# A 32-head attention block gated by a Mish MLP on one NeuronCore: four more places for the last W2 pieces, three first W1 pieces, and a reordered tail

## The chip, the core and the metric

The kernel runs on one core of a Trainium2 chip. The metric is the device time of one execution, in microseconds (us). A core has a TensorE (PE in the profile, with its weight loads as PEld), a VectorE (DVE), a ScalarE (ACT), a GpSimd (POOL) and a SyncE (SP), each with its own instruction queue that runs in order. SP issues nearly all DMAs here, so an SP instruction that waits holds back every DMA behind it. TensorE writes to PSUM, eight banks of 128 x 512 f32; everything else lies in SBUF tiles whose places are reused.

## The reference

```python
def _A_ref(x, wqkv, wo):                      # attention, 32 heads of 32
    q, k, v = ...                             # (x @ wqkv), split and transposed
    p = _softmax(jnp.einsum("bhqd,bhkd->bhqk", q, k) * (Dh ** -0.5))
    o = jnp.einsum("bhqk,bhkd->bhqd", p, v)
    return o.transpose(0, 2, 1, 3).reshape(B, S, D) @ wo

def _B_ref(x, w1, b1, w2):                    # dense, Mish, dense
    h = x @ w1 + b1
    return (h * jnp.tanh(softplus(h))) @ w2

x = A_x                                       # 1 x 2048 x 1024, f32
xn = _layernorm(x)
return x + _A_ref(xn, wqkv, wo) * silu(_B_ref(xn, w1, b1, w2))   # F = 3584
```

## The kernel before

The work is f32 throughout, and a product of two f32 matrices is made of three matmuls of rounded parts (high x high, high x low, low x high, the table `THREE`), so every operand is split first: ScalarE copies the high part, and VectorE or GpSimd subtracts it to leave the low part (`copy` L282, `low` L290). A matmul that needs the low part of its left operand comes third of its three.

The kernel has three phases. First come layernorm, the projections to Q, K and V, and the presplit W1 and W2, written to DRAM (lines up to 782; the scores of head 0 start there too). Then attention and MLP run together, L785 to L1426: five streams yield matmuls (scores for the row maxima `s`, scores for the exponentials `t`, first MLP layer `h` L1076, second MLP layer `y` L1217, and `p_stream`, the output projection `op` L1357), and the class `Plan`, a list scheduler with costs written by hand, decides at build time in which order each engine's instructions stand. Last comes a tail written by hand, L1429 to L1522.

Places are rings in the plan. `p` has 6 tiles of 128 x 2048 for exponentials (`PS`); an exponential's tile is given back when both its sum (POOL, L939) and its product with V (`pv`, L958; for the last two tiles the sum is a matmul, `zp`, L996) have used it. `w2` has 3 places for pieces of W2 (`W2S`), `w1` has 3 for pieces of W1. The MLP is made in units `U` and row chunks of 512; the second layer uses a Strassen-like scheme with 7 blocks `j` for a pair of units, two half-tiles `s` each, summed by VectorE into `yacc` (L1243). Two pieces of W2 serve a block, so the last pair of units uses pieces 378 to 391, blocks y_0 to y_6.

`p_stream` begins the projection inside the plan: it loads `wo` raw (`wr0` to `wr3`), splits it, loads the first row chunk's attention output (`or0`, `or1`, into `p` tiles, split into `xo`), and yields the eight output tiles of chunk 0 in two halves of the contraction, k = 0 to 3 and then k = 4 to 7. The head outputs go to DRAM in `ot` (L1018), the MLP outputs of each chunk in `ys` (L1284); the last chunk's `ys` store waits for the last `ot` store.

The tail works through chunks c = 0 to 3 of four row tiles t. Chunk 0's matmuls are in the plan already; for c = 1 to 3 each row tile takes two groups (dh = 0, 1) of 24 matmuls (`p_mm`). For them the attention output of the chunk is loaded (`new_o`, `oraw`) and split (`split_o`, `ohl` for odd chunks, `xo` for even ones). The MLP output is loaded (`y_load`, `yp`), its seven blocks are combined by seven POOL additions (`y_total`, L1465; done earlier for chunk 0), `silu` runs on ScalarE, and `end` multiplies the PSUM result by the gate (L1477), adds x (L1478) and stores it (L1482). The bank of a group is reused by the group one chunk later, once `end` has read it. ScalarE and VectorE run these in program order: a `silu` that waits for `y_total` holds back the copies behind it.

```python
    op_ = pool(ph, "op", 8)                   # L1430, over mlp and yacc
    yp = pool(ph, "yp", 2, side="right")      # L1433
    ...
    silu(0)                                   # L1492
    for k in range(4):
        split_o(1, k)                         # the other four are interleaved with end(t, dh), t < 4
```

Of the kernel before, what the change touches and what calls it, by code (L numbers as in the profile page):

```python
# [9 lines left out]
F32 = mybir.dt.float32  # L10
# [8 lines left out]
P = 128  # L19
KT = D // P  # L20
# [11 lines left out]

MM, PV = 0.22667, 0.8587

GROUPS, ZP = (4, 4, 4, 4), 2

LEAD, LATE = 8, 4.0

# [191 lines left out]
def body(ctx: ExitStack, tc: tile.TileContext, x, wqk, wv, wo, w1, b1, w2, out):  # L230
# [7 lines left out]
    def pool(stack, name, bufs, side="left", **kw):  # L238
        return stack.enter_context(tc.tile_pool(name=name, bufs=bufs, side=side, reuse_waits="tile", **kw))
# [363 lines left out]
    def load_head(h, parts=range(3)):  # L603
        r = slice(h % 4 * DH, h % 4 * DH + DH)
        q, k = qst[h % 3], kst[h % 3]
        if h > 2:
            move(q[96:98, :], zeros[0:2, :])
        elif h:
# [150 lines left out]
    for f in range(2 * KT):  # L759
        for c in range(NC):  # L760
            qk_group(f, c if f < 2 * KT - 1 else (c + 1) % NC)
            while todo and todo[0][0] <= f * NC + c:
                todo.pop(0)[1]()
            if c == 0 and f + 1 < 2 * KT:
                qk_split(f + 1)
                if f + 2 < 2 * KT:
                    later.at(1, lambda f=f + 2: qk_load(f))
            if f == 8 and c == 0:
                load_head(0)
            if f == 15 and c == 0:  # L770
# [14 lines left out]
    stk = pool(att0, "stk", 1, side="right")  # L785
    ps_a = psum(att0, "ps_a", 1)
    ph = ExitStack()
    mlp = pool(ph, "mlp", 1)
# [12 lines left out]
    def op(*args, **kw):  # L801
        return plan.add(Op(*args, **kw))
# [238 lines left out]
    def w1_op(n):  # L1041
        def emit(at):
            load_w1(n)
        w1_ops[n] = op("SP", 0.1, emit=emit, take=["w1"], bytes_=P * KT * P * 4)

    def w2_op(m, need=()):
        def emit(at):
            w2t[m] = mlp.tile([P, 2, 512], F32R, tag=f"w2{at['w2']}", name=f"w2_{m}")
# [12 lines left out]
    def h_stream():  # L1061
        for n in range(NC * FT):
            c, f = divmod(n, FT)
            if f == 0 and c + 1 < NC:
                xc_op(c + 1)
            t = {}
            i = 0
            for k in range(KT):
                m_ = 2 * n + k // 4
                if k % 4 == 0 and m_ + 2 < 2 * NC * FT:  # L1070
                    w1_op(m_ + 2)
                for a, b in THREE:
                    def mm(at, n=n, c=c, k=k, a=a, b=b, i=i, t=t, m_=m_):
                        if i == 0:
                            t["h"] = bank(at, f"h{n}")
                        nc.tensor.matmul(t["h"], w1t[m_][:, a, k % 4], xts_[c][:, b, k], start=i == 0, stop=i == 3 * KT - 1)  # L1076
                    last = i == 3 * KT - 1
                    due = n + (i + 1) / 24 - (AHEAD if n >= NC * FT - 2 else 0)
                    m = Op("PE", MM, key=tile_time * due, emit=mm,
                           need=([w1_ops[m_]] if n else []) + ([xc_ops[c, k // 2 * 2]] if c else []),  # L1080
                           take=["d", "b", "h"] if i == 0 else [],
                           give=(["w1"] if i % 12 == 11 else []) + (["xc"] if last and f == FT - 1 else []))
# [112 lines left out]
            act_ops[u, "z", 0].need.append(act_ops[u, "z", 1])  # L1195

    made_by, gs = {}, {}
    yacc = mlp.tile([P, 7, 2, 512], F32, name="yacc")

    def y_stream():  # L1200
        for m in range(W2S):
            w2_op(m, [m_there[0, 3]])
        free, freed = {}, [0]
        for B in range(0, NC * U, 2):
            c, b = divmod(B, U)
            done = {}
            for j, (kind, half) in enumerate(YSEQ):
                t = {}
                for n, (v, s) in enumerate(ORDER):
                    m_ = 7 * B + 2 * j + v  # L1210
                    for i, (p, q) in enumerate(THREE):
# [20 lines left out]
                        if "w2" in give and W2S + (at_ := freed[0]) < NC * U * 7:  # L1232
                            w2_op(W2S + at_)
                        freed[0] += "w2" in give
                        if not last:
                            continue

                        def y_add(at, j=j, s=s, b=b, t=t):
# [3 lines left out]
                            else:  # L1242
# [37 lines left out]

    def y_store(c, done):
        def store(j):
            return op("SP", 0.1, need=[done[j, i] for i in range(2)] + ([stored[H - 1]] if c == NC - 1 else []),
                      bytes_=P * 1024 * 4, emit=lambda at: nc.sync.dma_start(ys[c][:, j], yacc[:, j]))  # L1284

        return {j: store(j) for j in range(7)}

# [72 lines left out]
    def p_stream():  # L1360
# [57 lines left out]

    plan.take_now("w1")
    plan.take_now("w1", 1)  # L1420
    plan.take_now("xc")
    plan.take_now("mx", 1)
    loaded[1] = None
# [9 lines left out]
    yp = pool(ph, "yp", 2, side="right")  # L1433
    oraw = {}

    def new_o(c, k):
# [20 lines left out]

    def y_load(c, js):
        for j in js:
            yt[c, j] = yp.tile([P, 2, 512], F32, tag=f"y{j}", name=f"yp{c}_{j}", bufs=2 if j in BLOCK.values() else 1)  # L1460
            nc.sync.dma_start(yt[c, j], ys[c][:, j])

    def y_total(c):
# [9 lines left out]
    def end(t, dh):  # L1473
        c, s = divmod(t, 4)
        y = yt[c, BLOCK[s // 2, dh]][:, s % 2]
        r = slice(dh * 512, dh * 512 + 512)
        nc.vector.tensor_tensor(y, ps[t, dh], y, ALU.mult)  # L1477
        nc.vector.tensor_tensor(xt[t][:, r], xt[t][:, r], y, ALU.add)  # L1478
# [86 lines left out]
```

## Time and profile before

| | before |
|---|---|
| runs, us | 3377.39, 3377.81, 3380.06; median 3377.81 |
| profiled execution, us | 3378.12 |
| its span, us | 3376.3 (1.8 us of the execution lie around it) |
| DVE, ACT, POOL busy, us | 2505.0, 2059.6, 2741.2 |
| mean granted TensorE clock | 0.996 |

The span runs from the first to the last instruction. PE's time and its waits stand in the prediction's quotes. The granted clock is the share of full speed that TensorE was given; in a stretch of length L with mean clock c, (1 - c) x L is about what the lower clock cost.

### The profile page before, as it was taken

Reading aid. Unit: us, or ns where it says so; the run is one execution under the profiler, and the core shown is the slowest. Engines: PE = TensorE matmul, PEld = TensorE weight load, DVE = VectorE, ACT = ScalarE, POOL = GpSimd, SP = SyncE. Lnnn points to the kernel's source line nnn. Section 1 sums busy time; section 2 is a strip of 40 time slices with the busy share of each in tenths; the row PEclk is TensorE's granted clock in tenths of the full one; section 3 lists DMA queues with packets and bytes.
Section 4 is the critical chain, followed back from the end, with each engine's and each line's share of the span. In section 5 each row is a group of like instructions: output and inputs, shape, how many; then the busy total and the mean of one; then the engine's idle time right before and its main releaser. Section 6 shows DMA issues by size and latency. Waiting matters only on the chain. (4 is left out here: it accounts for less than half of the span.)

```text
span 3376.3 us, 47946 instructions
## 1 busy us (share of the span) xinstructions
PE 3334.9 (99%) x17123; PEld 2454.0 (73%) x17123; DVE 2505.0 (74%) x4126; ACT 2059.6 (61%) x3523; POOL 2741.2 (81%) x1061
## 2 busy tenths in 40 slices
PE   8999999999999999999999999999999999999999
PEld 8898887676677767767767777776776677776677
DVE  5024446888888888888888888888888888885464
ACT  6112122677777767777777777777776776777421
POOL 4557663889999999999999899998988989999442
PEclk9999999999999999999999999999999999999999
DMA  7999997545455565545555655555556545545673
GB/s 269 348 324 373 366 367 240 144 132 147 143 145 151 148 205 169 156 145 149 149 153 144 206 188 154 155 156 155 149 155 215 177 144 153 152 146 181 229 291 118
DMA packets 258467, 649.32 MB, mean 192 GB/s; under 512 B 90586, under 2 KB 99802, under 8 KB 249690
## 3 DMA queue, kind: packets, MB, share of 16 engines
q1 hardware_dynamic: 255780, 637.86, 59.8%
q10 hardware_dynamic: 2448, 8.39, 0.6%
q8 instruction: 136, 2.23, 0.3%
q14 instruction: 103, 0.84, 0.1%
HBM read 479.69 MB, written 165.41 MB: 191 GB/s over the span
## 5 line engine op out<-in xcount | busy, mean ns | idle before, releaser
L939 POOL TENSOR_TENSOR z<-z,p 128x2048 f32<-128x2048 f32 x446 | 2057.3, 4613 | 70.9 <-ACT p L279 46.7
L279 ACT ACTIVATE p<-t,zero 128x512 f32<-128x512 f32 x2048 | 1375.4, 689 | 403.8 <-PE t L910 392.1
L829 DVE TENSOR_REDUCE mx<-s 128x1 f32<-128x512 f32 x1984 | 1317.1, 685 | 181.2 <-PE s L823 176.0
L910 PE MATMUL t<-qstack,kstack 128*128 128x512 f32 x2048 | 801.6, 395 | 3.4 <-DMA qstack<-mt 2.7
L823 PE MATMUL s<-kstack,qstack 128*128 128x512 f32 x1984 | 775.3, 394 | 0.7 <-DMA w<-w1s 0.4
L1076 PE MATMUL h<-xr,w 128*128 128x512 f32 x2016 | 729.3, 390 | 0.1
L910 PEld LDWEIGHTS t<-qstack,kstack 128*128 128x128 f32 x2048 | 383.6, 188 | 135.5 <-issue 35.2
L958 PE MATMUL pv<-p,v 128*32 128x512 f32 x4096 | 467.7, 597 | 0.0
L823 PEld LDWEIGHTS s<-kstack,qstack 128*128 128x128 f32 x1984 | 371.7, 188 | 111.9 <-issue 13.4
L1076 PEld LDWEIGHTS h<-xr,w 128*128 128x128 f32 x2016 | 378.4, 188 | 84.6 <-issue 5.0
L745 PE MATMUL qk<-xc,qkw 128*128 128x512 f32 x1536 | 351.3, 390 | 0.3
L745 PEld LDWEIGHTS qk<-xc,qkw 128*128 128x128 f32 x1536 | 288.1, 188 | 60.7 <-DVE mx L627 1.2
L958 PEld LDWEIGHTS pv<-p,v 128*32 128x32 f32 x4096 | 120.5, 110 | 276.4 <-issue 252.9
L939 POOL TENSOR_TENSOR z<-p,p 128x2048 f32<-128x2048 f32 x32 | 147.9, 4622 | 149.2 <-PE zp L996 77.7
L1217 PE MATMUL y<-w,ay 128*128 128x512 f32 x672 | 250.6, 394 | 3.5 <-DMA w<-w2s 3.2
L1243 DVE TENSOR_TENSOR yacc<-yacc,y 128x512 f32<-128x512 f32 x336 | 228.4, 680 | 34.4 <-PE y L1217 33.5
L1217 PE MATMUL y<-w,az 128*128 128x512 f32 x672 | 250.4, 390 | 0.0
L1076 PE MATMUL h<-xc,w 128*128 128x512 f32 x672 | 247.3, 391 | 0.0
L1217 PE MATMUL y<-w,ax 128*128 128x512 f32 x672 | 246.0, 391 | 1.2 <-DMA w<-w2s 0.8
L1217 PEld LDWEIGHTS y<-w,ay 128*128 128x128 f32 x672 | 127.0, 189 | 32.1 <-issue 4.4
L1217 PEld LDWEIGHTS y<-w,ax 128*128 128x128 f32 x672 | 125.9, 188 | 31.7 <-issue 2.5
L1076 PEld LDWEIGHTS h<-xc,w 128*128 128x128 f32 x672 | 126.6, 189 | 26.6 <-DVE mx L627 0.2
(143 smaller groups left out, 3644.9 us busy)
## 6 DMA issues: line engine op xcount, KB each, us to landing
w<-w2s SPq DMA_DIRECT2D x392, 512.0 KB
w<-w1s SPq DMA_DIRECT2D x224, 512.0 KB
w2s<-pw SPq DMA_DIRECT2D x98, 512.0 KB
qstack<-qs SPq DMA_DIRECT2D x96, 256.0 KB
kstack<-ks SPq DMA_DIRECT2D x96, 256.0 KB
w1s<-w1h SPq DMA_DIRECT2D x36, 512.0 KB
qs<-qst SPq DMA_DIRECT2D x32, 512.0 KB
ks<-qst SPq DMA_DIRECT2D x32, 512.0 KB
```

Source lines behind the costliest of these rows:

```text
L279: nc.scalar.activation(out_, in_, fn, bias=zero if bias is None else bias, scale=scale)
L745: nc.tensor.matmul(ps, w[:, k // 4, a, k % 4], xc[c][:, b, k], start=n == 0, stop=n == 3 * KT - 1)
L823: nc.tensor.matmul(sp_, qst[h % 3][:, qt * P:(qt + 1) * P], kst[h % 3][:, kc * 512:(kc + 1) * 512], start=True, stop=True)
L829: nc.vector.reduce_max(tiles["mx"][:, qt, kc:kc + 1], tiles[qt, kc], axis=AX.X)
L910: nc.tensor.matmul(tp, kst[h % 3][:, kt * P:(kt + 1) * P], qst[h % 3][:, c * 512:(c + 1) * 512], start=True, stop=True)
L939: nc.gpsimd.tensor_tensor(zs[h], pts[T - 1] if kt == 1 else zs[h], pts[T], ALU.add)
L958: nc.tensor.matmul(t["b"][c * DH:(c + 1) * DH, :], vt[h][:, k, :], pts[T - kt + k][:, c * 512:(c + 1) * 512], start=k == kt - size + 1, st ...
L1076: nc.tensor.matmul(t["h"], w1t[m_][:, a, k % 4], xts_[c][:, b, k], start=i == 0, stop=i == 3 * KT - 1)
L1217: nc.tensor.matmul(t["y", s], acts[A, kind, half][:, p, s * P:(s + 1) * P], w2t[m_][:, q], start=first, stop=last)
L1243: nc.vector.tensor_tensor(ya, ya, t["y", s], ALU.subtract)
```

## The change

Four things are changed.

1. `w2_grow` takes a `p` tile when the last head's exponentials are done, and makes two more W2 places of it; `p_stream` calls it twice (`GROW`). With them, seven W2 pieces can be held. The other loads that take `p` tiles (`wr2`, `wr3`, `or1`) get later ones.
2. `load_w1` is called for three pieces ahead of the plan, not two, and the plan's first `w1_op` is left out. Head 2's constant rows (96 and up of `qst[2]`, `kst[2]`) are written by three GpSimd memsets, where two DMAs wrote them.
3. `yacc` lives in a pool of its own that outlives the plan. The last chunk's `ys` stores leave the plan and stand in the tail, behind the loads for chunk 0; the `yp` pool opens in yacc's place after them, with one buffer per block, and the even chunks' four gate blocks lie in a pool `yq`.
4. In the tail all eight `split_o(1, k)` stand ahead of `silu(0)`, `op_` lies on the right side (over the `p` tiles), and `end` keeps the product in PSUM and adds it from there.

```diff
@@ ahead of the plan
-                load_w1(0)
-                load_w1(1)
+                for n in range(3):
+                    load_w1(n)
...
+    yacc = pool(ya, "ya", 1).tile([P, 7, 2, 512], F32, name="yacc")
...
+    nc.gpsimd.memset(qst[2][96:P, :].bitcast(F32), 0.0)
+    nc.gpsimd.memset(kst[2][96:P, :].bitcast(F32), 0.0)
+    nc.gpsimd.memset(kst[2][96:98, :].bitcast(F32), 1.0)
@@ w2 places
+    w2_more, w2_next = {}, [W2S]
+
+    def w2_grow():
+        def emit(at):
+            n = W2S + len(w2_more)
+            t = att.tile([P, 2, 2, 512], F32R, tag=f"p{at['p']}", name=f"w2more{n}")
+            for i in range(2):
+                w2_more[n + i] = t[:, i]
+                plan.rings["w2"].append((plan.at["SP"], n + i))
+                if w2_next[0] < NC * U * 7:
+                    w2_op(w2_next[0])
+                    w2_next[0] += 1
+
+        op("SP", 0.02, emit=emit, take=["p"])
@@ y_stream
-            while c == NC - 1 and b == U - 2 and H - 1 not in stored:
-                yield None
             if b == U - 2:
-                free = (y_store if c else y_sums)(c, done)
+                free = y_sums(c, done) if c == 0 else y_store(c, done) if c < NC - 1 else {}
@@ p_stream
         o_raw("or0", range(4))
         wo_raw("wr2", (4, 5), in_p("wr2"), take=["p"])
+        for i in range(GROW):
+            w2_grow()
@@ tail
-    op_ = pool(ph, "op", 8)
+    op_ = pool(ph, "op", 8, side="right")
...
-        nc.vector.tensor_tensor(y, ps[t, dh], y, ALU.mult)
-        nc.vector.tensor_tensor(xt[t][:, r], xt[t][:, r], y, ALU.add)
+        nc.vector.tensor_tensor(ps[t, dh], ps[t, dh], y, ALU.mult)
+        nc.vector.tensor_tensor(xt[t][:, r], xt[t][:, r], ps[t, dh], ALU.add)
...
     y_load(0, (3, 5))
+    for j in range(7):
+        nc.sync.dma_start(ys[NC - 1][:, j], yacc[:, j])
+    ya.close()
+    yp = pool(ph, "yp", 1)
     start(2)
     start(3)
+    for k in range(KT):
+        split_o(1, k)
     silu(0)
-    for k in range(4):
-        split_o(1, k)
...
-                if c + 1 < NC and (c or k > 3):
+                if c and c + 1 < NC:
                     split_o(c + 1, k)
```

On TensorE the order is the same, row for row, up to the end of the last pair of units. There, just behind the second layer's block y_2, the order before was as follows (`op` is the projection with its `wo` and `xo`, `w_384` to `w_386` are W2 pieces):

```order
L1357 MATMUL op_0_31774<-wo_30207,xo_31713 128x512 x3
L1357 MATMUL op_0_31774<-wo_30920,xo_31713 128x512 x3
L1357 MATMUL op_0_31774<-wo_0_31666,xo_31713 128x512
L1357 MATMUL op_0_31774<-wo_1_31676,xo_31713 128x512
L1357 MATMUL op_0_31774<-wo_0_31666,xo_31713 128x512
L1357 MATMUL op_0_31774<-wo_31746,xo_31713 128x512 x3
L1217 MATMUL y_3_0_31813<-w_384_31752,ay_54_31385 128x512 x3
L1217 MATMUL y_3_1_31817<-w_384_31752,ay_54_31385 128x512 x3
L1357 MATMUL op_1_31821<-wo_30207,xo_31713 128x512 x3
```

On TensorE at the same place, the changed kernel has this:

```order
L1373 MATMUL op_0_31784<-wo_30211,xo_31717 128x512 x3
L1236 MATMUL y_3_0_31795<-w2more_31737,ay_54_31389 128x512 x3
L1236 MATMUL y_3_1_31800<-w2more_31737,ay_54_31389 128x512 x3
L1373 MATMUL op_0_31784<-wo_30924,xo_31717 128x512 x3
L1236 MATMUL y_3_0_31795<-w2more_31737,ay_55_31688 128x512 x3
L1236 MATMUL y_3_1_31800<-w2more_31737,ay_55_31688 128x512 x3
L1373 MATMUL op_0_31784<-wo_0_31670,xo_31717 128x512
L1373 MATMUL op_0_31784<-wo_1_31680,xo_31717 128x512
L1373 MATMUL op_0_31784<-wo_0_31670,xo_31717 128x512
L1373 MATMUL op_0_31784<-wo_31756,xo_31717 128x512 x2
```

Two groups of six second-layer matmuls have moved in between the projection's first three k, where before all twelve projection matmuls stood in a row.

On SP, in the same stretch, the order of the DMAs before was (`or` and `wr` are the raw loads of the projection, `w_384` and on the W2 pieces):

```order
L1304 DMA wr_31733<-in_A_wo_dram 128x1024
L1304 DMA or_31735<-ot_131 128x512
L1304 DMA wr_31664<-in_A_wo_dram 128x1024
L286 DMA w_384_31752<-w2s_122 128x1024
L286 DMA w_385_31765<-w2s_123 128x1024
L286 DMA w_386_31779<-w2s_122 128x1024
L1304 DMA wr_31733<-in_A_wo_dram 128x1024
```

On SP it is now:

```order
L286 DMA w2more_31737<-w2s_122 128x1024
L286 DMA w2more_31737<-w2s_123 128x1024
L286 DMA w2more_31738<-w2s_122 128x1024
L286 DMA w2more_31738<-w2s_123 128x1024
L1320 DMA wr_31668<-in_A_wo_dram 128x1024
L1320 DMA wr_31750<-in_A_wo_dram 128x1024
L1320 DMA or_31752<-ot_131 128x512
L286 DMA w_388_31762<-w2s_122 128x1024
```

Pieces 384 to 387 now stand where `wr3`'s first load stood (it is `wr_31733` before and `wr_31750` now), ahead of three raw loads and not behind them.

On ACT, where the tail begins, the order before was (`ohl` are the copies of chunk 1's split, `yp` is `silu`):

```order
L279 ACT_TABLE_LOAD
L279 ACTIVATE yp_0_32131<-yp_0_32131,zero 128x512
L279 ACTIVATE yp_4_32133<-yp_4_32133,zero 128x512
L282 ACTIVATE ohl_0_32105<-oraw_0_32106 128x512
L282 ACTIVATE ohl_1_32108<-oraw_1_32109 128x512
```

On ACT it is now:

```order
L282 ACTIVATE ohl_5_32114<-oraw_5_32115 128x512
L282 ACTIVATE ohl_6_32117<-oraw_6_32118 128x512
L282 ACTIVATE ohl_7_32120<-oraw_7_32121 128x512
L279 ACT_TABLE_LOAD
L279 ACTIVATE yp_0_32125<-yp_0_32125,zero 128x512
```

All eight copies of chunk 1 now stand ahead of the first `silu`, which waits for its MLP output.

More of the change, by code (lines that the diff above doesn't have):

```diff
@@ L33 @@
 MM, PV = 0.22667, 0.8587
-GROUPS, ZP = (4, 4, 4, 4), 2
+GROUPS, ZP, GROW = (4, 4, 4, 4), 2, 2
 LEAD, LATE = 8, 4.0
@@ L607, in load_head @@
             move(q[96:98, :], zeros[0:2, :])
-        elif h:
+        elif h == 1:
             move(q[96:P, :], zeros)
@@ L787, in body @@
     ph = ExitStack()
+    ya = ExitStack()
+    yacc = pool(ya, "ya", 1).tile([P, 7, 2, 512], F32, name="yacc")
     mlp = pool(ph, "mlp", 1)
@@ L1044, in w1_op @@
         w1_ops[n] = op("SP", 0.1, emit=emit, take=["w1"], bytes_=P * KT * P * 4)
+    w2_more, w2_next = {}, [W2S]
[10 more added lines that the diff above has]
+        op("SP", 0.02, emit=emit, take=["p"])
     def w2_op(m, need=()):
         def emit(at):
-            w2t[m] = mlp.tile([P, 2, 512], F32R, tag=f"w2{at['w2']}", name=f"w2_{m}")
+            n = at["w2"]
+            w2t[m] = w2_more[n] if n in w2_more else mlp.tile([P, 2, 512], F32R, tag=f"w2{n}", name=f"w2_{m}")
             move(w2t[m], w2s[(m // 14 * 2 + m % 2) % U][:, m % 14 // 2])
@@ L1069, in h_stream @@
                 m_ = 2 * n + k // 4
-                if k % 4 == 0 and m_ + 2 < 2 * NC * FT:
+                if k % 4 == 0 and 2 < m_ + 2 < 2 * NC * FT:
                     w1_op(m_ + 2)
@@ L1079, in h_stream @@
                     m = Op("PE", MM, key=tile_time * due, emit=mm,
-                           need=([w1_ops[m_]] if n else []) + ([xc_ops[c, k // 2 * 2]] if c else []),
+                           need=([w1_ops[m_]] if m_ > 2 else []) + ([xc_ops[c, k // 2 * 2]] if c else []),
                            take=["d", "b", "h"] if i == 0 else [],
@@ L1197, in body @@
     made_by, gs = {}, {}
-    yacc = mlp.tile([P, 7, 2, 512], F32, name="yacc")
     def y_stream():
@@ L1202, in y_stream @@
             w2_op(m, [m_there[0, 3]])
-        free, freed = {}, [0]
+        free = {}
         for B in range(0, NC * U, 2):
@@ L1231, in y_stream @@
                         yield m
-                        if "w2" in give and W2S + (at_ := freed[0]) < NC * U * 7:
-                            w2_op(W2S + at_)
-                        freed[0] += "w2" in give
+                        if "w2" in give and w2_next[0] < NC * U * 7:
+                            w2_op(w2_next[0])
+                            w2_next[0] += 1
                         if not last:
@@ L1282, in store @@
         def store(j):
-            return op("SP", 0.1, need=[done[j, i] for i in range(2)] + ([stored[H - 1]] if c == NC - 1 else []),
-                      bytes_=P * 1024 * 4, emit=lambda at: nc.sync.dma_start(ys[c][:, j], yacc[:, j]))
+            return op("SP", 0.1, need=[done[j, i] for i in range(2)], bytes_=P * 1024 * 4, emit=lambda at: nc.sync.dma_start(ys[c][:, j], yacc[:, j]))
         return {j: store(j) for j in range(7)}
@@ L1420, in body @@
     plan.take_now("w1", 1)
+    plan.take_now("w1", 2)
     plan.take_now("xc")
@@ L1429, in body @@
     ph = ExitStack()
-    op_ = pool(ph, "op", 8)
+    op_ = pool(ph, "op", 8, side="right")
     rp = pool(ph, "rp", 8, side="right")
     xp = pool(ph, "xp", 5, side="right")
-    yp = pool(ph, "yp", 2, side="right")
+    yq = pool(ph, "yq", 1, side="right")
     oraw = {}
@@ L1459, in y_load @@
         for j in js:
-            yt[c, j] = yp.tile([P, 2, 512], F32, tag=f"y{j}", name=f"yp{c}_{j}", bufs=2 if j in BLOCK.values() else 1)
+            where = yq if c % 2 == 0 and j in BLOCK.values() else yp
+            yt[c, j] = where.tile([P, 2, 512], F32, tag=f"y{j}", name=f"yp{c}_{j}")
             nc.sync.dma_start(yt[c, j], ys[c][:, j])
```

## The prediction

> **What bounds the kernel now.** The page first: its span, and the busy share of each engine.
>
> ```profile
> span 3376.3 us, 47946 instructions
> ...
> PE 3334.9 (99%) x17123; PEld 2454.0 (73%) x17123; DVE 2505.0 (74%) x4126; ACT 2059.6 (61%) x3523; POOL 2741.2 (81%) x1061
> ```
>
> TensorE (PE) is busy for 99% of the span, and the change takes no matmul away. So it can win only where PE waits or runs at a lower clock, and the next view is the list of PE's waits (us in total, times, longest).
>
> ```profile
> PE y L1217 <- DMA w<-w2s: 7.0, 5, 3.2
> PE op L1357 <- DVE ohl L290: 4.1, 2, 3.6
> PE op L1357 <- DVE xo L290: 3.6, 2, 3.3
> PE t L910 <- DMA qstack<-mt: 2.7, 1, 2.7
> PE op L1357 <- ACT ohl L282: 2.4, 1, 2.4
> ...
> PE s L823 <- DMA w<-w1s: 0.4, 1, 0.4
> ```
>
> These six come to 20.2 us. PE's timeline places them (start, us, what ran; in brackets the wait ahead and who ended it):
>
> ```profile
> 3170.15 0.96 PE L1357 MATMUL op<-wo,xo 128*128 128x512 f32 x3 [3.34 <-DVE xo L290]
> ...
> 3190.78 1.63 PE L1217 MATMUL y<-w,aw 128*128 128x512 f32 x6 [0.28 <-DMA w<-w2s]
> 3194.70 1.84 PE L1217 MATMUL y<-w,aw 128*128 128x512 f32 x6 [2.30 <-DMA w<-w2s]
> ...
> 3237.12 1.22 PE L1357 MATMUL op<-wo,ohl 128*128 128x512 f32 x2 [2.43 <-ACT ohl L282]
> ...
> 3244.36 39.95 PE L1357 MATMUL op<-wo,ohl 128*128 128x512 f32 x169 [3.57 <-DVE ohl L290]
> ```
>
> All the projection's waits and two of those for W2 lie between 3165 and 3245 us, where the change works. The windows show what they cost (busy time and count of PE, PEld, DVE, ACT, POOL; then granted clock, DMA share, GB/s; PEld's count is that of the matmuls).
>
> ```profile
> 3165.50:3196.30 30.80, 24.63 (x97) 18.96 (x96) 15.78 (x22) 5.82 (x9) 2.34 (x1) 0.94 0.71 229
> 3194.70:3199.60 4.90, 4.89 (x14) 3.89 (x15) 1.38 (x2) 0.00 (x0) 0.00 (x0) 0.65 1.02 416
> 3196.30:3230.40 34.10, 34.10 (x145) 28.08 (x144) 13.77 (x18) 9.65 (x15) 5.81 (x3) 0.95 0.97 368
> 3230.40:3284.10 53.70, 47.20 (x193) 37.32 (x193) 34.76 (x31) 12.01 (x20) 31.72 (x12) 0.90 0.74 264
> 3237.10:3241.00 3.90, 3.17 (x5) 1.29 (x5) 3.86 (x3) 1.83 (x3) 3.90 (x3) 0.50 0.52 179
> 3284.10:3371.40 87.30, 87.25 (x385) 71.92 (x384) 37.14 (x40) 13.54 (x22) 18.59 (x7) 1.00 0.35 133
> ```
>
> The last window is undisturbed: 87.30 us for 384 matmuls, 0.2273 us each, at full clock. At that rate 3165.5 to 3196.3 (A, 96 matmuls) needs 21.8 of its 30.8 us, an excess of 9.0; 3196.3 to 3230.4 (B, 144) 32.7 of 34.1, excess 1.4; 3230.4 to 3284.1 (C, 192) 43.6 of 53.7, excess 10.1. Together **20.5 us**. The waits are 3.6 + 0.28 + 2.30 = 6.2 in A and 4.1 + 2.4 = 6.5 in C. The lower clock adds 0.06 x 30.8 = 1.8, 0.05 x 34.1 = 1.7 and 0.10 x 53.7 = 5.4. The short windows show where: 0.65 right behind the wait of 2.30, 0.50 behind that of 2.43. The clock loss therefore belongs to the waits, and I let it go with them.
>
> The Trainium skill ("TensorE: Matmul & The Clock Gate", section "HAM oscillation — how this bites in real kernels") gives as its rule that idle gaps over about 3.4 us bring the clock down. Here gaps of 2.30 and 2.43 us were enough; by the page's rule those dips would have another cause and stay, which is the third rival.
>
> **The W2 places.** Here are SP's DMA issues, the last three with their counts.
>
> ```profile
> 3157.84 0.33 SPq L1304 DMA_DIRECT2D wr<-in_A_wo_dram  x1
> ...
> 3162.95 3.07 SPq L286 DMA_DIRECT2D w<-w2s  x3
> ...
> 3189.53 8.09 SPq L1284 DMA_DIRECT2D ys<-yacc  x7
> 3197.71 6.09 SPq L1444 DMA_DIRECT2D oraw<-ot  x8
> ```
>
> Pieces 384 to 387 are issued from about 3157.8 now, where the order has them ahead of `wr3`, and not from 3162.95; the last four then follow into the first three places as these come free, earlier than in before, where only three places turned over. y_3 and y_4 move in between the projection's k groups, into the wait of 3.34. The two W2 waits of A go: -2.6 with the clock behind them. What pays is the split of wo and xo:
>
> ```profile
> 3167.76 2.33 DVE L290 TENSOR_TENSOR xo<-or,xo 128x512 fp32r<-128x512 f32 x1
> ...
> 3178.22 1.22 DVE L290 TENSOR_TENSOR wo<-wr,wo 128x1024 fp32r<-128x1024 f32 x1
> ...
> 3189.85 1.37 DVE L1243 TENSOR_TENSOR yacc<-yacc,y 128x512 f32<-128x512 f32 x2 [2.03 <-PE y L1217]
> ...
> 3227.40 0.68 DVE L1477 TENSOR_TENSOR yp<-op,yp 128x512 f32<-128x512 f32 x1
> 3228.11 2.17 DVE L1478 TENSOR_TENSOR x<-x,yp 128x512 f32<-128x512 f32 x1
> 3230.20 2.88 DVE L290 TENSOR_TENSOR ohl<-oraw,ohl 128x512 fp32r<-128x512 f32 x1
> ...
> 3246.79 0.69 DVE L290 TENSOR_TENSOR xo<-oraw,xo 128x512 fp32r<-128x512 f32 x1 [1.16 <-ACT xo L282]
> ```
>
> ```profile
> 3167.20 2.34 POOL L290 TENSOR_TENSOR wo<-wr,wo 128x1024 fp32r<-128x1024 f32 x1 [4.31 <-ACT wo L282]
> ...
> 3261.25 19.24 POOL L1465 TENSOR_TENSOR yp<-yp,yp 128x1024 f32<-128x1024 f32 x7 [17.49 <-DMA yp<-ys]
> ```
>
> The same subtraction takes 0.69 us alone and 2.33 under POOL's `wo` subtraction of 2.34, which stays. So a small wait for xo_1 or xo_2 remains: at least 0.5 us; at most the 3.6 less the first y_3 group of six (1.4), 2.1. I take **+1.4**, near the middle. `wr3` and `or1` now come later, since their `p` places are free only behind the last sums. wo_7's low part stands on DVE behind the additions of y_6, so it ends at about y_6's end + 1.37 + 1.22, and the last xo about 2 us later. With A at 21.8 + 1.4, y_6 ends at 3188.7, wo_7 at 3191.3, xo_7 at 3193.4. PE first needs them some 13 us behind y_6, at 3201.7; 8 us of slack, cost 0. If that cover were gone, each us over would be a us.
>
> **The third W1 piece and head 2's constants.**
>
> ```profile
> 581.42 1.31 SPq L286 DMA_DIRECT2D w<-w1s  x1
> ```
>
> W1's piece 2 was issued at 581.42 and now goes with the first two, ahead of the plan. PE's waits at the start are 0.4 us for W1, 2.7 for `qstack<-mt` and 3.2 for W2; only the first is for a W1 piece, and the other two stand behind DMAs that the change leaves. POOL gets three memsets in place of two DMAs for which PE never waits.
>
> ```profile
> L583 POOL MEMSET qstack<- x1: 1804/1804/1804, 210.9 to 210.9; 32x2048 f32 x1
> ```
>
> ```profile
> 592.22 4.62 POOL L939 TENSOR_TENSOR z<-p,p 128x2048 f32<-128x2048 f32 x1 [38.31 <-ACT p L279]
> ```
>
> Three of about 1.8 us (an estimate from this row; one is two rows high) lie in POOL's 38.31 idle us: 0 where that cover holds, 5.4 where it does not. Value 0; at best SP gets to the wait of 2.7 sooner: -2.7, and 1.7 of clock as behind the 2.30, -4.4.
>
> **The tail.** Chunk 1's splits stood between `silu` and `end` on ACT and DVE, so a copy waited for `end`, that for `y_total`, that for DMAs:
>
> ```profile
> 3212.86 1.28 ACT L279 ACT_TABLE_LOAD   x1 [27.22 <-DMA yp<-ys]
> ...
> 3236.44 0.63 ACT L282 ACTIVATE ohl<-oraw 128x512 fp32r<-128x512 f32 x1 [9.67 <-DVE x L1478]
> ```
>
> Now all eight stand first. Their loads, 8 x 256 KB, wait on SP behind the place that wo_7's raw tile leaves (3191.3); at B's 368 GB/s that is 5.7 us, and the splits end by about 3201. Chunk 1 starts at 3188.7 + 32.7 = 3221.4, so there are 20 us of slack: C's 6.5 of waits and their clock go. B's 1.4 goes with the wait of 2.30 ahead of it.
>
> What is late next is `y_total(1)`. Its blocks lie in yacc's place now, behind the seven stores of `ys`.
>
> ```profile
> ys<-yacc SPq DMA_DIRECT2D x25, 512.0 KB
> ...
> oraw<-ot SPq DMA_DIRECT2D x24, 256.0 KB
> ```
>
> From 3191.3 SP's queue holds six `oraw` (256 KB), and twenty of 512 KB: stores, loads of x and loads of blocks, with about 1 MB of output beside them, 13.1 MB. At 368 GB/s (B, where the queue was full too) that is 35.6 us, to 3227. POOL takes 19.24 / 7 = 2.75 us for an addition, and five of them pass before the first gate of chunk 1: 3240.6. From there DVE does eight groups of L1477, L1478 and a split of chunk 2, 3 x 0.69 = 2.1 each, and waits four times 1.1 for the copy: 21.2 us, last split at 3261.8. If each split were held like the 2.88 above, 17.6 more: 3279.4. PE comes to chunk 2 at 3221.4 + 43.6 = 3265.1 and needs the last split 21 matmuls later, at 3269.9. So the cost lies between 0 and 9.5. POOL's 19.24 us cover about 19.24 / (2.1 + 2.2) = 4.5 groups, which gives 3271.7: 1.8 us of wait, and **+2.0** with a little clock.
>
> `end` now adds x from PSUM. The rows above show the reading of PSUM (L1477) at 0.68 and the SBUF sum (L1478) at 2.17 while POOL ran, so I count the new sum at 0.69: already in the 2.1; at 2.17 it would be inside the 9.5.
>
> The Trainium skill ("SBUF — State Buffer", section "Who interferes with whom") says that a VectorE instruction with two SBUF inputs contends with a GpSimd instruction that reads SBUF, and one with at most one does not. These rows agree with it; by it the split stays slow and the sum becomes fast.
>
> **The sum.** 3376.3 - 20.5 + 1.4 + 2.0 = 3359.2 of span; 3378.1 - 3376.3 = 1.8 lie around it: **3361.0 us**. The profiled execution, 3378.12, is 0.3 above the median of the runs, which is within their own spread.
>
> **The rivals.** *First, chunk 2's splits stall PE further*: all eight held by POOL, 9.5 in place of 2.0, so 3368.5 (from 3366 up). For it: 2.88 and 2.17 stand in before; against: POOL's work is 19.24 us long, not 38. *Second, the start gains too*, as piece 2's earlier place frees SP: 3361.0 - 4.4 = 3356.6; against it, both waits name other DMAs. *Third, the clock dips are not the waits' doing and stay*: 1.8 + 1.7 + 5.4 = 8.9 back, 3369.9; against it, the 0.65 and 0.50 right behind waits. *Fourth, the change does not do what it says*: the `p` places come free too late for the W2 pieces, A keeps its 9.0 and something takes C's place: 3371 to 3378. *Fifth, slower*: blocks 1 to 6 of chunk 1 queue behind the `ys` stores, and the queue moves A's 229 GB/s, not B's 368. Then 13.1 MB takes 57 us, to 3248.5, the first gate comes 13.7 later at 3262.2, and the last split of chunk 2 31.1 later, 3293.3: a wait of 23.4 in place of 1.8, so 3382.6. It decides where the wait passes 18.7, the loads end at 3243.8, which is 250 GB/s. Against it, B and the 416 right behind 3194.7 are from the same queue when full, and A's 229 from one that was not.
>
> **How the numbers follow.** The forecast, 3357 to 3366, has 0.60; the first rival 0.20, the second 0.05, the third 0.06, the fourth 0.05, the fifth 0.04. The range, 3357 to 3369, holds the forecast and the first rival to its end. A change of 0.2%, 6.8 us, is about what a measurement of this kernel can tell, so faster begins below 3371. Faster: 0.60 + 0.20 + 0.05 + 0.02 of the third = 0.87; within 0.2%: 0.04 of the third and the fourth, 0.09; slower 0.04.
>
> **What would show it.** In the changed profile PE's list should have no wait of `op` for `ohl` and none for `w2s` after 3165 us; the windows from there should show a clock near 1.00; chunk 1's `ohl` copies on ACT should stand ahead of the table load; the sum with x should take 0.69 us under POOL. The waits for `qstack<-mt` (2.7) and for the first W2 pieces (3.2) should be unchanged. A wait for `xo` where chunk 2 begins, much over 2 us, is the first rival; loads of `yp` that land after 3240, the fifth; a lower clock with no wait ahead of it, the third. I am wrong if the W2 wait at y_6 remains.

## The result, and the profile after

| | before | after |
|---|---|---|
| median of 6 runs, us | 3378.14 (3374.33 to 3380.06) | 3357.89 (3355.60 to 3359.66) |
| profiled execution, us | 3378.12 | 3356.72 |
| its span, us | 3376.3 | 3354.9 |
| mean granted TensorE clock | 0.996 | 0.999 |

The ratio is 0.9941, with a 95% interval of 0.9928 to 0.9954: the change takes 20 us, 0.6%. The forecast of 3361.0 lies 3.1 us above the median, and the median lies in the range of 3357 to 3369.

PE is again busy for 99% of the span, on the same 17123 matmuls. Its busy time fell from 3334.9 to 3326.3 us because fewer of them ran at a lower clock.

```profile
span 3354.9 us, 47948 instructions
...
PE 3326.3 (99%) x17123; PEld 2450.9 (73%) x17123; DVE 2481.5 (74%) x4126; ACT 2060.8 (61%) x3523; POOL 2742.0 (82%) x1064
```

In the list of PE's waits after (us in total, times, longest) `op` no longer waits for `ohl` at all, and 0.3 us are left of its 3.6 us for `xo`. The two stops at the start are still there, the one for `qstack<-mt` with 3.2 in place of 2.7 and the first one for W2 with 1.9 in place of 3.2; the prediction had both unchanged.

```profile
PE y L1236 <- DMA w<-w2s: 4.7, 4, 1.9
PE t L915 <- DMA qstack<-mt: 3.2, 1, 3.2
...
PE op L1373 <- DVE xo L290: 0.3, 1, 0.3
```

The windows of after answer to those of before. They begin at the first projection matmul behind the W2 block, at the second half of chunk 0, at chunk 1 and at chunk 2 (busy time and count of PE, PEld, DVE, ACT, POOL; granted clock, DMA share, GB/s).

```profile
3163.96:3186.35 22.39, 22.06 (x98) 17.95 (x97) 10.89 (x18) 7.30 (x11) 2.40 (x1) 1.00 0.68 255
3186.35:3218.99 32.64, 32.64 (x146) 27.05 (x145) 16.47 (x25) 10.48 (x15) 0.00 (x0) 1.00 0.90 342
3218.99:3262.51 43.52, 43.52 (x194) 36.06 (x193) 19.05 (x27) 9.93 (x16) 27.20 (x12) 1.00 0.94 350
3262.51:3349.50 86.99, 86.99 (x385) 71.85 (x383) 31.60 (x41) 14.78 (x24) 24.86 (x10) 1.00 0.42 147
```

Every window has the clock at 1.00. The first took 30.8 us in before and 22.4 now, chunk 1 took 53.7 and takes 43.5. PE's timeline shows one wait left between 3160 us and the end.

```profile
3166.95 0.50 PE L1373 MATMUL op<-wo,xo 128*128 128x512 f32 x1 [0.33 <-DVE xo L290]
...
3186.35 32.80 PE L1373 MATMUL op<-wo,xo 128*128 128x512 f32 x144
3218.99 43.68 PE L1373 MATMUL op<-wo,ohl 128*128 128x512 f32 x192
3262.51 17.68 PE L1373 MATMUL op<-wo,xo 128*128 128x512 f32 x77
```

PE's matmuls come in the same order in both kernels but for 27 places in the last units, so the time between the same two matmuls can be set side by side. Five stretches are used from here on, each counted from matmul to matmul in the trace: S1, 35 matmuls around the stop for `qstack<-mt` near 582 us; S2, 30 matmuls around the first stop for W2 near 668; A, 115 matmuls from 3161.4 us of before (the last W2 blocks, the projection's first half and the first two matmuls of its second half); B, the next 144 (its second half, two matmuls late); C, the next 192 (chunk 1, likewise). Undisturbed, A, B and C would take 26.1, 32.7 and 43.6 at 0.2273 us each.

| us | S1 | S2 | A | B | C |
|---|---|---|---|---|---|
| before | 12.6 | 10.8 | 35.8 | 33.7 | 53.7 |
| after | 13.4 | 8.5 | 26.9 | 32.6 | 43.5 |
| difference | +0.8 | -2.3 | -8.9 | -1.1 | -10.2 |

A, B and C give 20.1 us before rounding, S1 and S2 1.5 more, and with small differences elsewhere the span is 21.4 shorter.

### The profile page after: what moved, and what is told of

It is laid out like the page before. It is cut to its first block, busy times and chain, and to the rows that moved or that the text cites. A ratio compares the mean times of both kernels' runs of the same rounds, so it can differ in the third digit from the quotient of the medians.

```text
span 3354.9 us, 47948 instructions
## 1 busy us (share of the span) xinstructions
PE 3326.3 (99%) x17123; PEld 2450.9 (73%) x17123; DVE 2481.5 (74%) x4126; ACT 2060.8 (61%) x3523; POOL 2742.0 (82%) x1064
## 4 chain that ended last, share of the span: by engine, by line
PE 94%; DMA 2%; POOL 1%; issue 1%; DVE 1%; ACT 1%; SPq 0%; POOLq 0%; DVEq 0%; ACTq 0%
PE h L1097 18%; PE y L1236 16%; PE t L915 14%; PE s L828 13%; PE pv L963 13%; PE qk L745 9%; PE op L1373 5%; PE v L331 5%; PE zp L1001 1%; DMA w<-w2s 1%; POOL pw L290 1%; PE pt L443 0%; POOL tmp L709 0%; DVE mx L834 0%; ACT p L279 0%
## 5 line engine op out<-in xcount | busy, mean ns | idle before, releaser
L828 PEld LDWEIGHTS s<-kstack,qstack 128*128 128x128 f32 x1984 | 371.6, 188 | 111.6 <-issue 13.4
L1262 DVE TENSOR_TENSOR yacc<-yacc,y 128x512 f32<-128x512 f32 x336 | 228.3, 680 | 30.8 <-PE y L1236 29.8
```

The costliest lines, as they stand in the source:

```text
L828: nc.tensor.matmul(sp_, qst[h % 3][:, qt * P:(qt + 1) * P], kst[h % 3][:, kc * 512:(kc + 1) * 512], start=True, stop=True)
L1262: nc.vector.tensor_tensor(ya, ya, t["y", s], ALU.subtract)
```

## The experiments

There are twelve runs, one of them (e9) of the changed kernel unaltered; "median" is that of the executions, and the ratio is to runs of the kernel before on the same chip. The stretches come from one trace of each.

| run | median, us (runs) | before, us | ratio and interval | S1 | S2 | A | B | C |
|---|---|---|---|---|---|---|---|---|
| e1 | 3365.5 (8) | 3376.6 | 0.9971 (0.9960 to 0.9981) | 14.6 | 8.5 | 34.5 | 32.6 | 43.5 |
| e2 | 3367.4 (9) | 3376.6 | 0.9977 (0.9967 to 0.9986) | 12.0 | 6.7 | 26.9 | 32.6 | 54.6 |
| e3 | 3373.2 (11) | 3376.6 | 0.9992 (0.9984 to 1.0001) | 15.0 | 6.5 | 26.9 | 32.6 | 58.5 |
| e4 | 3364.7 (5) | 3376.6 | 0.9967 (0.9954 to 0.9979) | 12.0 | 8.1 | 36.2 | 33.5 | 43.5 |
| e5 | 3355.6 (5) | 3377.2 | 0.9933 (0.9920 to 0.9947) | 13.7 | 7.1 | 27.6 | 32.6 | 43.5 |
| e6 | 3357.5 (5) | 3377.2 | 0.9943 (0.9930 to 0.9955) | 14.2 | 9.3 | 26.9 | 32.6 | 43.5 |
| e7 | 3359.9 (5) | 3377.2 | 0.9944 (0.9932 to 0.9957) | 13.3 | 9.8 | 26.9 | 32.6 | 43.5 |
| e8 | 3359.4 (5) | 3377.2 | 0.9946 (0.9933 to 0.9958) | 14.6 | 9.0 | 26.9 | 32.6 | 43.5 |
| e9 | 3358.9 (5) | 3375.4 | 0.9952 (0.9940 to 0.9965) | 14.5 | 8.9 | 27.7 | 32.6 | 43.5 |
| e10 | 3356.0 (5) | 3375.4 | 0.9943 (0.9929 to 0.9957) | 13.7 | 8.9 | 26.9 | 32.6 | 43.5 |
| e11 | 3379.5 (11) | 3375.4 | 1.0011 (1.0002 to 1.0020) | 14.1 | 9.3 | 35.0 | 32.6 | 56.0 |
| e12 | 3362.5 (5) | 3375.4 | 0.9960 (0.9948 to 0.9973) | 13.3 | 9.6 | 31.6 | 32.6 | 43.5 |

### e1 and e2: the W2 places taken away, and alone

e1 is the changed kernel without its places:

```diff
-GROUPS, ZP, GROW = (4, 4, 4, 4), 2, 2
+GROUPS, ZP, GROW = (4, 4, 4, 4), 2, 0
```

> The changed kernel without its four W2 places (all else kept). Theory: the places are worth what stretch A and the start of B gained in the two traces (8.4 us in A, 1.5 in B), so the waits of y_5 and y_6 for w2s and the one of op for xo come back with a clock near 0.65 behind them: 3366 to 3368 us. Rival: it is the later place of wr3 and or1 and the earlier tail that freed A, and the W2 pieces would have come in time: 3358, no w2s wait after 3160.

e2 is the kernel before with `w2_grow` and the two calls in `p_stream`:

```diff
         wo_raw("wr2", (4, 5), in_p("wr2"), take=["p"])
+        for i in range(GROW):
+            w2_grow()
```

> The kernel before with the four W2 places and nothing else. Theory: gains add up, A and B give 8.4 + 1.5 us and C keeps its 10.1: 3368 us (3366 to 3370). Rival: C's waits hang on DMAs (the ys stores and the loads behind them) that do not come sooner when PE does, so C takes the gain back: 3372 to 3378, with waits for ohl of more than 6.5 us.

e1 gave 3365.5, 7.7 above the changed kernel's median and half a us under the theory's bounds; against the kernel before on the same chip e1 saves 11.0 us, and the changed kernel 20.3 (16.5 in e9). Its A is 34.5 where the changed kernel has 26.9, and these are the waits in its timeline of PE:

```profile
3170.14 0.98 PE L1373 MATMUL op<-wo,xo 128*128 128x512 f32 x3 [3.36 <-DVE xo L290]
...
3190.75 1.60 PE L1236 MATMUL y<-w,aw 128*128 128x512 f32 x6 [0.28 <-DMA w<-w2s]
3194.03 1.65 PE L1236 MATMUL y<-w,aw 128*128 128x512 f32 x6 [1.67 <-DMA w<-w2s]
```

They are those of before (3.34, 0.28 and 2.30) but for a shorter last one, so the rival, that the tail's other edits free A, falls. No clock was lost behind the 1.67, though: B is 32.6, and the 1.5 us that the theory had for it did not come. e2 gave 3367.4, as the theory said: A is 26.9 without any of the other edits. C did not take the gain back in time (54.6 for 53.7), though its waits for `ohl` are 7.0 in e2's list and were 6.5 (4.1 and 2.4):

```profile
PE op L1373 <- ACT ohl L282: 4.6, 2, 2.7
...
PE op L1373 <- DVE ohl L290: 2.4, 3, 1.0
```

### e3 and e4: the order of chunk 1's splits undone, and alone

e3 is the changed kernel with

```diff
-    for k in range(KT):
-        split_o(1, k)
     silu(0)
+    for k in range(4):
+        split_o(1, k)
...
-                if c and c + 1 < NC:
+                if c + 1 < NC and (c or k > 3):
```

> The changed kernel with chunk 1's splits where they were (four behind the first silu, four between end's), all else kept. Theory: the last copies stand on ScalarE behind the gate of row tile 4, which waits for GpSimd's sums until about 3235, while chunk 1 needs them by 3224: PE waits some 12 us and loses 3 or more to the clock: 3371 to 3376. Rival: what helped C is the places and the stores' new position, not the order: 3358 to 3360.

e4 is the kernel before with the same edit the other way round, and nothing else.

> The kernel before with all eight splits of chunk 1 ahead of the first silu and nothing else. Theory: C's waits for ohl and their clock go (10.1 us): 3368 (3366 to 3371). Rival: with the old places the raw loads come too late (SP issues them from 3197.7, behind the ys stores), the silu's behind the splits are late for the banks, and part of the gain is lost: 3372 to 3378.

Both theories held in their mechanism. In e3 PE stands 11.74 us at chunk 1, and ScalarE's timeline shows behind what: the copy of the last `ohl` follows a `silu` that waited for GpSimd.

```profile
3234.93 1.22 PE L1373 MATMUL op<-wo,ohl 128*128 128x512 f32 x2 [11.74 <-ACT ohl L282]
```

```profile
3226.50 0.72 ACT L279 ACTIVATE yp<-yp,zero 128x512 f32<-128x512 f32 x1 [6.51 <-POOL yp L1485]
3233.64 0.72 ACT L279 ACTIVATE yp<-yp,zero 128x512 f32<-128x512 f32 x1 [6.41 <-POOL yp L1485]
3234.26 0.61 ACT L282 ACTIVATE ohl<-oraw 128x512 fp32r<-128x512 f32 x1
```

With it the whole change is worth almost nothing (ratio 0.9992): PE comes to chunk 1 at 3218.3 and not at 3230.5, but the gate that the copy stands behind is ready only at 3233.6. In the changed kernel the same two kinds of rows stand the other way round, the copies first and the wait for GpSimd behind them, where it holds nobody back:

```profile
3197.11 1.29 ACT L282 ACTIVATE ohl<-oraw 128x512 fp32r<-128x512 f32 x2 [1.58 <-DMA oraw<-ot]
3198.41 1.28 ACT L279 ACT_TABLE_LOAD   x1
...
3228.07 0.72 ACT L279 ACTIVATE yp<-yp,zero 128x512 f32<-128x512 f32 x1 [16.51 <-DMA yp<-ys]
3235.35 0.73 ACT L279 ACTIVATE yp<-yp,zero 128x512 f32<-128x512 f32 x1 [6.56 <-POOL yp L1485]
```

e4 takes C to 43.5 with before's places, stores and loads. Its median is 1.3 us below the theory's bounds, 11.8 under before's; against before's trace 10.2 come from C and 3.3 from S1 and S2, where the edit does nothing, and A is 0.4 longer.

### e5 and e11: the third W1 piece and head 2's constants, undone and alone

e5 is the changed kernel with two W1 pieces ahead of the plan and the constants by DMA; e11 is the kernel before with

```diff
-                load_w1(0)
-                load_w1(1)
+                for n in range(3):
+                    load_w1(n)
...
+    nc.gpsimd.memset(qst[2][96:P, :].bitcast(F32), 0.0)
+    nc.gpsimd.memset(kst[2][96:P, :].bitcast(F32), 0.0)
+    nc.gpsimd.memset(kst[2][96:98, :].bitcast(F32), 1.0)
```

> The changed kernel with two W1 pieces ahead of the plan and head 2's constants by DMA, as in before. Theory, from five traces: the third piece does not help PE; with it the wait for qstack<-mt near 582 was 3.2, 3.2 and 3.7 us (changed kernel and two variants), without it 2.7, 1.9 and 1.8, so undoing it leaves the time or gains up to 2 us: 3356 to 3358, that wait at 1.8 to 2.7. Rival: the 1.6 us by which the changed kernel led at the start of the last units are this part's: 3359 to 3361, and the w2s wait near 668 back at 3.2.

> The kernel before with the third W1 piece and the three memsets and nothing else. Theory: nothing to win, perhaps 1 to 2 us lost at the wait for qstack<-mt: 3377 to 3380. Rival: the start gains what the changed kernel led by at 3165 us, 1.6: 3375 to 3376.

Alone this part makes the kernel slower: 1.0011, interval 1.0002 to 1.0020, which is 3.7 us (0.7 to 6.8). Without it the changed kernel comes to 3355.6, half a us below what the theory expected; its interval overlaps the changed kernel's. S1 has 12.0 to 13.7 us, mean 12.8, in the five traces without this part (before, e2, e4, e5, e10) and 13.3 to 15.0, mean 14.1, in the nine with it. So there is no sign that it helps. By the means about 1.3 us of what it costs lies at S1, but there is one trace of each and the two sets overlap; the rest can't be told from the scatter, nor was it tried whether the piece or the memsets cost it. In e5 the wait near 582 fell to 2.3, as the theory said, and S1 was no shorter than the changed kernel's. S2 is no part of it: with before's own start it was 10.8, 6.7, 8.1, 7.1 and 8.9, with the new one 6.5 to 9.8. The 2.3 us that the changed kernel's trace won there lie within that scatter.

### e6, e7 and e8: the other parts of the tail

e6 is the changed kernel with the product back in SBUF:

```diff
-        nc.vector.tensor_tensor(ps[t, dh], ps[t, dh], y, ALU.mult)
-        nc.vector.tensor_tensor(xt[t][:, r], xt[t][:, r], ps[t, dh], ALU.add)
+        nc.vector.tensor_tensor(y, ps[t, dh], y, ALU.mult)
+        nc.vector.tensor_tensor(xt[t][:, r], xt[t][:, r], y, ALU.add)
```

> The changed kernel with end as before: the product goes back to SBUF and x is added from there. Theory: under GpSimd's sums that addition takes 2.2 us and not 0.69, some four times in chunk 1 and four in chunk 2; DVE has that much room, and the last split of a chunk is set by ScalarE behind the silu, so 0 to 2 us more: 3358 to 3360. Rival: the longer additions push the last split of chunk 2 past its matmul, and each us counts: 3362 to 3366 with a wait of op for xo at about 3267.

3357.5, half a us under the theory's bounds, and PE has no wait that the changed kernel hasn't (0.3 for `xo` in both): the theory's mechanism holds, and the rival falls. The addition itself is three times as long under GpSimd's sums, as VectorE's timeline of e6 shows (first) beside that of the changed kernel (second):

```profile
3239.06 0.68 DVE L1497 TENSOR_TENSOR yp<-op,yp 128x512 f32<-128x512 f32 x1
3239.77 2.17 DVE L1498 TENSOR_TENSOR x<-x,yp 128x512 f32<-128x512 f32 x1
```

```profile
3238.16 0.69 DVE L1497 TENSOR_TENSOR op<-op,yp 128x512 f32<-128x512 f32 x1
3238.88 0.69 DVE L1498 TENSOR_TENSOR x<-x,op 128x512 f32<-128x512 f32 x1
```

So the edit does what it can do for VectorE, and VectorE has no need of it.

e7 moves the second copy of each row tile ahead of the `silu`:

```diff
-                if c and c + 1 < NC:
-                    split_o(c + 1, k)
+                if c and c + 1 < NC and dh == 0:
+                    split_o(c + 1, k)
+                    split_o(c + 1, k + 1)
```

> The changed kernel with both copies of a row tile ahead of the next silu in chunks 1 and 2. Theory: in the changed kernel the last split of chunk 2 ends at 3267.6, when its matmul is due, behind a silu that waits for GpSimd; now it ends near 3260. PE did not wait there in the profile, so 0 to 1 us: 3357 to 3358. Rival: in other runs than the profiled one PE does wait there, and the median falls by 1 to 2 us, to 3356.

3359.9 from runs of 3354.2 to 3361.5: inconclusive, and it bears out neither. Its profiled run was one of the long ones, and lost 4.9 us against the changed kernel's trace before 3165, where the edit does nothing; from A on the two agree within 0.1 us.

e8 puts the last `ys` stores back into the plan:

```diff
-    for j in range(7):
-        nc.sync.dma_start(ys[NC - 1][:, j], yacc[:, j])
...
+                free = (y_store if c else y_sums)(c, done)
```

> The changed kernel with the last ys stores back in the plan, ahead of the tail's loads. Theory: SP then issues the oraw loads some 9 us later, behind the stores (until about 3196); chunk 1's splits end near 3207, still ahead of 3219, and the first silu near 3210, ahead of the bank that chunk 1 needs at 3219: 3357 to 3360. Rival: the later first gate holds up end and with it the banks, or the splits are late: waits of op between 3219 and 3240, 3362 to 3368.

3359.4, and A, B and C as in the changed kernel: moving the stores is worth nothing here.

### e9, e10 and e12: the changed kernel again, two edits alone, and half the places

> The changed kernel once more, unaltered, beside the next three on the same chip: 3355 to 3360, for comparison with them.

e10 is e2 and e4 together, the kernel before with the places and the order of the splits only.

> The kernel before with the four W2 places and with chunk 1's splits ahead of the first silu, and nothing else of the change: two W1 pieces, constants by DMA, ys stores in the plan, op on the left, end through SBUF. Theory: these two edits are the whole gain (each alone gave 9 and 12 us, the other parts undone one at a time gave 0 to -2): 3354 to 3358. Rival: the parts that cost nothing one at a time stand in for each other (later stores, places on the left and end through SBUF together delay chunk 2): 3360 to 3366, with a wait of op for xo or ohl after 3215.

3356.0 beside 3358.9 for the changed kernel on the same chip. The intervals overlap, so e10 can't be called the faster one; but it has all of the gain, and the rest of the change is not needed for it.

e12 is the changed kernel with one more tile, two places:

```diff
-GROUPS, ZP, GROW = (4, 4, 4, 4), 2, 2
+GROUPS, ZP, GROW = (4, 4, 4, 4), 2, 1
```

> The changed kernel with two more W2 places (one tile) in place of four. Theory: y_3's two pieces come in time, y_4 to y_6 turn over five places; y_3 still fills the wait for xo, and at most the last piece (391) is late: 3358 to 3362, one w2s wait of up to 2 us after 3165. Rival: all four are needed, and the waits of A come back: 3364 to 3367.

3362.5, just over the theory's bounds, and neither mechanism: no wait for W2 is left after 3165, yet A is 31.6. What came back is the wait for `xo`. PE, VectorE and GpSimd of e12:

```profile
3163.18 1.29 PE L1373 MATMUL op<-wo,xo 128*128 128x512 f32 x5
3167.82 0.50 PE L1373 MATMUL op<-wo,xo 128*128 128x512 f32 x1 [3.34 <-DVE xo L290]
3168.16 4.52 PE L1236 MATMUL y<-w2more,ay 128*128 128x512 f32 x12
```

```profile
3165.43 2.33 DVE L290 TENSOR_TENSOR xo<-or,xo 128x512 fp32r<-128x512 f32 x1
```

```profile
3164.86 2.35 POOL L290 TENSOR_TENSOR wo<-wr,wo 128x1024 fp32r<-128x1024 f32 x1 [4.36 <-ACT wo L282]
```

And PE, VectorE and GpSimd of the changed kernel at the same place (PE's wait there is the 0.33 shown above, at 3166.95):

```profile
3164.64 1.52 PE L1236 MATMUL y<-w2more,ay 128*128 128x512 f32 x6
```

```profile
3166.21 0.68 DVE L290 TENSOR_TENSOR xo<-or,xo 128x512 fp32r<-128x512 f32 x1
```

```profile
3169.33 2.40 POOL L290 TENSOR_TENSOR wo<-wr,wo 128x1024 fp32r<-128x1024 f32 x1 [8.55 <-DMA w<-w2s]
```

Two things turn the 0.33 into 3.34. The first six matmuls of y_3, 1.36 us, stand ahead of the waiting matmul in the changed kernel and behind it in e12, so it was wrong that y_3 still fills the wait. And the split takes 2.33 in place of 0.68, 1.65 more: with four places GpSimd's subtraction starts three us behind VectorE's, with two it starts ahead of it and holds it, as in before. (In the changed kernel it starts when ScalarE's copies end, at about 3169.25; it reads no W2, so the DMA in its bracket is not what it waits for.) So what the second tile's two places are worth is in about equal parts the six matmuls that cover the wait and the later time to which they push another engine's work. That the raw `wo` loads, which stand behind four W2 pieces on SP and not behind two, are what pushes it is likely, but was not tried apart. 31.6 - 26.9 = 4.7 us: 3.0 more of wait, and 1.7 of clock behind it (0.66 over 5 us).

## Why the prediction was right, point by point

**The bound and the sizes of A, B and C.** Right. 9.0, 1.4 and 10.1 us of excess were counted from the waits and the clock behind them; 8.9, 1.1 and 10.2 went (A here takes in two matmuls of the second half, 0.4 us that the prediction had in B). e2 and e4 show the causes apart, 9.2 and 11.8 us on the medians, and their sum of 21.0 is that of e10 (19.4) and of the change (16.5 to 20.3) within the scatter.

**The clock goes with the waits.** Right on the whole: no window of the changed kernel after 3165 us is below 1.00, and in all 14 traces the clock falls between 575 us and the last matmul only in or behind a wait of 1.7 us or more. With the waits of e3 and e12 a loss came back; with e1's 1.67 none did, so not every wait has its price in clock. The third rival, and with it the rule of 3.4 us in the Trainium skill ("TensorE: Matmul & The Clock Gate", section "HAM oscillation — how this bites in real kernels"), would have kept 8.9 us; the traces do not agree with it. The 8.9 itself was too large. The 5.4 for C counts the clock through the wait of 3.57 too, when PE had nothing to run:

```profile
3240.79:3244.36 3.57, 0.00 (x1) 0.00 (x0) 3.57 (x3) 0.00 (x0) 2.97 (x2) 0.50 0.92 292
```

Without that half of 3.57 it is 3.6, and the three terms come to 7.1. The forecast does not use them, since it takes the excess whole.

**The wait for xo, +1.4.** Too large. 0.33 us are left, and A gained 8.9 us where the sum had 9.0 - 1.4 = 7.6. The step that failed is "under POOL's `wo` subtraction of 2.34, which stays": it does not stay at that place. The subtraction starts at 3169.33, behind VectorE's, and the split takes 0.68. That y_3's first six matmuls fill 1.4 of the wait was right. e12 shows the other case of both. The margin is small, though: waits of 0.98 in e5 and 1.10 in e9 stood there, and A was 27.6 and 27.7.

**Chunk 2's start, +2.0.** Too large, but the place was the right one. In the changed kernel the last split of chunk 2 starts at 3265.99 and takes 1.59, so it ends at 3267.6, just when its matmul is due; in e9 it was late.

```profile
3265.99 1.59 DVE L290 TENSOR_TENSOR xo<-oraw,xo 128x512 fp32r<-128x512 f32 x1 [7.30 <-DMA oraw<-ot]
```

```profile
3223.16 17.33 POOL L1485 TENSOR_TENSOR yp<-yp,yp 128x1024 f32<-128x1024 f32 x7 [51.43 <-DMA yp<-ys]
3252.17 17.68 POOL L1485 TENSOR_TENSOR yp<-yp,yp 128x1024 f32<-128x1024 f32 x7 [11.68 <-DMA yp<-ys]
```

```profile
3270.76 38.61 PE L1373 MATMUL op<-wo,xo 128*128 128x512 f32 x169 [0.79 <-DVE xo L290]
```

The first fence is VectorE and the second GpSimd in the changed kernel, the third PE in e9. The sum counted on a first gate at 3240.6, five additions of 2.75 behind the loads; GpSimd began at 3223.16, took 17.33 / 7 = 2.48 for each, and had the five done when ScalarE's row above starts at 3235.35. It also let GpSimd's sums lie over 4.5 splits; four of the eight fell into the gap between the two sums, from 3240.5 to 3252.2, and a split that was held took 1.5 to 1.6 and not 2.88. The last one is late for another reason than the one given: its copy stands on ScalarE behind a `silu` of chunk 2, which waits for the second sum. The split starts as that copy ends, at 3265.96; the copy reads the same raw tile, so the DMA in the bracket is not what the split waited for.

```profile
3264.71 0.72 ACT L279 ACTIVATE yp<-yp,zero 128x512 f32<-128x512 f32 x1 [6.58 <-POOL yp L1485]
3265.34 0.62 ACT L282 ACTIVATE xo<-oraw 128x512 fp32r<-128x512 f32 x1
```

The slower rival (loads at 229 GB/s) did not come: chunk 1's window moved 350.

**The third W1 piece, 0.** Wrong by a little: alone it costs 3.7 us (0.7 to 6.8), some 1.3 of them at S1. For the waits at the start the prediction had bounds of -4.4 and 0; the only loss it named was 5.4 if the memsets did not fit into GpSimd's idle time, and no PE wait names a memset. What costs the time stays open. The 1.6 us that the profiled execution had gained ahead of 3165 lie within the scatter of S2: e2 and e4, which have before's start, gained there too.

**Stores, op_ and end.** Counted at 0 to within the chunk 2 term, and e6, e8 and e10 bear that out.

Taken together: 1.3 us too much for xo, 2.0 for chunk 2 and 1.5 gained ahead of 3165, less 0.3 by which B gained less, come to 4.5; the forecast and the profiled execution (3361.0 and 3356.7) are 4.3 apart; the median of the runs is 1.2 above that execution. The errors did not cancel: the median lies 0.9 us above the lower end of the range, and the 1.5 at the start is luck of two single executions.

## What to carry to other kernels

On an engine that is busy for 99% of the span, waits of 2 to 3 us cost about one and a half times themselves in the sum, since the clock falls behind most of them (20.5 us for 12.7 of waits here, 4.7 for the 3.0 that e12 waits longer): price a stretch against its matmuls at the full rate, not by its waits. Where a queue runs in program order, put the work that feeds the bounding engine ahead of an instruction that waits for a slow producer; that one edit of a few lines gave half of the gain here, and without it nearly all of the other half was lost again. Of a change with many parts try the parts alone: two edits have all of this one, and one of the others seems to cost a little.

## What the runs showed of the hardware

How short a gap can bring the clock down was not expected, nor that a longer one can leave it alone. In the changed kernel PE waited 1.86 us for W2 at 666.57, and from 667.70 on ran at 0.53 for 3.5 us; behind another wait, of 1.61 at 3151.80, the clock stayed at 1.00.

```profile
666.57 0.70 PE L1236 MATMUL y<-w,ay 128*128 128x512 f32 x2 [1.86 <-DMA w<-w2s]
```

```profile
3151.80 0.94 PE L1236 MATMUL y<-w,ax 128*128 128x512 f32 x3 [1.61 <-DMA w<-w2s]
```

```profile
667.70:671.20 3.50, 3.50 (x21) 0.91 (x24) 2.64 (x5) 2.57 (x6) 0.73 (x1) 0.53 0.66 265
```

```profile
3151.80:3158.00 6.20, 6.20 (x46) 2.97 (x50) 4.73 (x7) 3.50 (x8) 4.24 (x4) 1.00 0.97 345
```

e1's wait of 1.67 at 3194.03 cost no clock either: its B is 32.6. But no limit of length between the two explains it. e11 waited 2.67 us for the last W2 piece, where before waited 2.30 and ran at 0.65 behind it, and its clock stayed at 1.00 (first fence); e4's wait of 1.72 near 666 was followed by 0.51 (second fence).

```profile
3195.02 1.65 PE L1220 MATMUL y<-w,aw 128*128 128x512 f32 x6 [2.67 <-DMA w<-w2s]
3195.00:3200.00 5.00, 4.98 (x22) 4.13 (x23) 1.38 (x2) 0.00 (x0) 0.00 (x0) 1.00 1.02 419
```

```profile
666.25 0.70 PE L1217 MATMUL y<-w,ay 128*128 128x512 f32 x2 [1.72 <-DMA w<-w2s]
667.70:671.20 3.50, 3.50 (x20) 0.87 (x16) 2.32 (x5) 2.75 (x6) 0.73 (x1) 0.51 0.54 217
```

In all 14 traces the clock of these stretches (from 500 us to the last matmul) is either 1.00 or 0.50, and each stretch at 0.50 lasts 3.41 us or two, three or four times that. So whether a wait of about 2 us costs 1.7 us of clock or none is not set by its length alone; what else sets it was not tried.

A wait five times as long cost only 1 us more of clock: behind e3's 11.74 us the windows show 0.50 for 3.6 us and 0.73 for 3.5 more, 0.5 x 3.6 + 0.27 x 3.5 = 2.7 us; behind before's 2.30 it was 0.35 x 4.9 = 1.7.

```profile
3234.90:3238.50 3.60, 3.20 (x7) 2.09 (x8) 2.85 (x3) 0.23 (x1) 3.60 (x2) 0.50 0.81 287
3238.50:3242.00 3.50, 3.50 (x13) 2.81 (x12) 2.59 (x4) 2.14 (x4) 0.19 (x1) 0.73 0.44 170
```

The stretch S2 took 6.5 to 10.8 us in 14 traces that run the same matmuls there, and single executions of the changed kernel lie 4 us apart: a us or two gained in one trace is no evidence.
